# Loading queries, keys and factors with one 128-row transfer per unit in a fused recurrence and Fourier-mixing kernel

## The chip, the cores and the metric

The kernel runs on one core of one Trainium2 chip. The metric is device time in microseconds (us) of one execution, lower is better. The kernel before took 546.61 us (median of 3 runs, 544.95 to 550.81).

## The reference

Two blocks in a row. The first is a gated linear recurrence over 768 tokens for 4 batches, 8 heads and a head width of 48; the second mixes its output with a two-dimensional Fourier transform and a feed-forward layer.

```python
# q, k, v, f_logit: (4, 8, 768, 48)
f = 1 / (1 + exp(-f_logit))
for t in range(S):
    state = f[:, :, t, :, None] * state + einsum('bhd,bhe->bhde', k[:, :, t], v[:, :, t])
    y[:, :, t] = einsum('bhd,bhde->bhe', q[:, :, t], state)

x = y.transpose(0, 2, 1, 3).reshape(4, 768, 384)
mixed = real(fft(fft(x, axis=1), axis=2))
u = x + mixed
un = (u - mean(u)) / sqrt(var(u) + 1e-6)          # over the last axis
out = u + maximum(un @ w_ch1, 0) @ w_ch2          # 384 -> 1536 -> 384
```

## The kernel before, in words

**Units.** Two heads of one batch make a unit, so that there are 16 units, four to a batch. The host hands queries, keys and factor logits over as one array `qkf` with the tokens innermost: for each unit and each of its two heads 48 rows, and in each row 768 tokens of q, then of k, then of f. On the chip a unit's q, k and f are three tiles of 128 rows by 768 tokens: head 0 in rows 0 to 47, head 1 in rows 64 to 111. Rows 48 to 63 are a gap that the matmuls don't read but that the elementwise operations, which run over rows 0 to 111 at once, do.

**Loads** (`load`, line 162). All are issued by SyncE's queue, in the order of the list of steps. A tile of q, k or f comes by two loads of 48 rows each (line 180). The gap of each buffer is filled once, at the start: the factors' four buffers with 30.0 on GpSimd (line 137), the seven buffers of keys and queries on VectorE (`gap`, line 132). There are four buffers for factors (`g_t`), three for keys (`k_t`) and four for queries (`q_t`), used in turn. The values' tile has six chunks of 128 tokens; it comes by three loads, and in its last three chunks the two halves of 64 tokens change places (lines 169 to 171).

**Attention** (`attention`, line 332, and `outputs`). For a unit: exponential and logarithm of the factors on ScalarE (lines 340, 341), a running sum over the tokens on VectorE that starts anew at each chunk (`W`, line 347), the decay over each chunk into `deep` (line 348 for five chunks on VectorE, line 349 for the sixth on GpSimd), two more exponentials (lines 352, 353), the products with queries and keys on VectorE (line 359, and lines 361 and 362 for keys, in two halves because the second one swaps the halves of its chunks), scores on TensorE (line 370), a causal mask (line 374), then products with values (line 528), the rest of the scores (line 545), the chunk states (lines 565, 573, 582), and a turn of the result into token rows `x` (line 602). The keys are turned separately (`keys_turned`, line 507), by a step of their own.

**Token fold** (`fold`, lines 613 to 653). As soon as a unit's part of `x` is there, its token chunks are folded into sums and differences for the Fourier transform. For the last unit of a batch all is on VectorE; for the other three, four of the seven operations (lines 629, 633, 634, 635) are on GpSimd.

**Fourier transform, projections.** When the four units of a batch are folded, `fnet` transforms them (`z`, line 691; `mix`, line 710) and normalizes; `turn` turns the rows for the projections (line 749). `projected` does the two projections for three pairs of token chunks: first 36 matmul calls `up` with the first matrix (line 791), then 42 calls `fx` and `fz` (line 814) with the second, in seven products of blocks. A matmul call in 32-bit floats appears as two instructions in the profile.

**Weights.** The two matrices come as 64-bit floats. Each is loaded in blocks of 384 KB into three `raw` buffers (24 blocks, line 277) and brought to 32 bits by VectorE, ScalarE and GpSimd together (lines 248 to 252). Later they are read a second time into free buffers of keys and factors (`reread`, line 303), for a check of their size.

**The order.** One list of words, `ORDER`, sets the order in which the steps of all this are written, and with it the order on every engine's queue: each engine, SyncE's queue of loads among them, takes its instructions strictly in that order. A number is the next step of that unit, `K` and a number turns that unit's keys, `F`, `H` and `P` with a number are the next step of the transform, the normalization and the projections of that batch, `L` loads (`L12qv`: the queries and values of unit 12), `r` and `R` load blocks of weights, `C` converts one, `V` and `c` read and check them again, `T` loads and `S` sorts the tables of the transform, `D` is eight matmuls without use that keep TensorE's clock up, `I`, `i` and `Z` set constants, `M` is the final judgement of whether a slower, exact path has to follow.

The list was written by a planner outside the kernel. The table loads of `T` (lines 185 to 201) are not touched by the change; one of them, line 199, loads 97 rows of 1,536 bytes.

Of the kernel before, what the change touches and what calls it, by code (L numbers as in the profile page):

```python
# [12 lines left out]
C = 128  # L13
# [6 lines left out]
KEEP = 2.0 ** 20  # L20
# [8 lines left out]
    "I D Gq0 D L0f Gk2 D L1f Gk1 D i D 0 Gk0 D D L0v L0q Gq2 D 1 Gq3 0 D 0 Gq1 D L0k 1 D L1q L2f Z D 1 0 "  # L29
    "D 0 2 K0 L1k D 0 0 2 L2q r L2k 1 D 0 0 L3fk 1 2 L1v D 3 0 K1 1 1 L3q 2 L4fk 0 3 1 L2v 2 C 1 4 r r 1 "  # L30
    "K2 2 2 1 0 4 3 C 2 L5fk 3 L3v D D r 5 2 D 3 2 K3 3 1 3 L4qv 5 4 2 L5qv C 3 4 C 4 R 4 3 D T 5 3 5 K4 "
    "2 L6fk C 5 C S 3 2 3 4 K5 r 3 5 4 D C F0 F0 6 F0 4 6 F0 L6qv C 4 6 F0 r 5 4 r H0 H0 L7fk C r 5 H0 6 "
    "7 5 F0 r P0 6 C C 7 L7qv 5 r K6 P0 P0 7 P0 6 C 7 6 C L8fk r r 5 F0 P0 6 r 6 C 8 C P0 L9fk C r P0 7 6 "
    "P0 9 H0 P0 r H0 7 8 7 C r K7 L9qv P0 r 7 9 C 7 9 6 P0 r L8qv 9 P0 C 9 7 9 C K9 C r P0 P0 8 H0 r 8 P0 "
    "r C L10fk 7 9 8 L11qv C L10qv 9 C 9 10 P0 P0 9 H0 P0 P0 5 W P0 6 L11fk P0 P0 P0 8 7 P0 6 P0 P0 P0 4 "
    "10 8 K8 P0 P0 P0 8 11 7 H0 P0 8 P0 P0 P0 P0 10 P0 P0 P0 P0 10 P0 F1 P0 P0 P0 P0 P0 P0 11 11 F1 L12fk "
    "8 10 K10 P0 P0 12 P0 11 10 F1 P0 F1 P0 L12qv L13fk F1 P0 10 11 H1 10 H1 H1 10 F1 P0 12 13 12 P0 P0 "
    "11 P0 P0 P0 P0 P0 P1 F1 8 P1 H1 L13qv K11 10 9 P1 8 P1 12 P1 P1 P1 H1 11 12 11 H1 P1 12 P1 11 9 P1 "
    "13 K12 P1 P1 P1 13 13 P1 10 P1 11 K13 L14fk P1 V L15fk P1 10 11 P1 P1 12 P1 10 13 15 12 H1 P1 P1 P1 "
    "P1 12 P1 12 L14qv H1 P1 11 P1 11 F2 F2 P1 14 14 P1 F2 13 P1 F2 P1 13 F2 P1 13 H2 V P1 P1 P1 15 14 P1 "  # L40
    "P1 P1 P1 P1 P1 c P1 P1 13 P1 14 14 13 K14 P1 V P1 P1 14 P1 F2 P1 14 P1 P1 H2 c P1 c F2 L15qv P1 P1 "
    "P1 P1 P1 P1 15 V P1 H2 V V H2 14 P1 H2 P2 P2 c P2 P2 P2 c P2 15 14 c 12 P2 V V c c P2 P2 P2 14 15 V "
    "V 13 P2 15 V 15 K15 P2 15 H2 P2 P2 P2 V 15 P2 P2 P2 c P2 13 P2 P2 P2 c P2 14 P2 15 H2 14 P2 P2 P2 V "
    "P2 P2 H2 15 P2 P2 P2 P2 P2 P2 P2 P2 14 c V P2 P2 P2 P2 15 12 c P2 c P2 P2 P2 P2 15 P2 V F3 P2 F3 F3 "
    "c P2 V F3 c c P2 F3 P2 P2 F3 P2 F3 P2 H3 P2 P2 P2 P2 P2 H3 P2 H3 H3 H3 P3 P3 P3 P3 P3 P3 P3 P3 P3 P3 "
    "P3 V P3 P3 P3 P3 H3 P3 P3 V P3 P3 c c P3 P3 P3 V V V c P3 P3 P3 P3 P3 P3 P3 P3 c H3 c H3 P3 P3 V P3 "
    "P3 P3 V P3 P3 P3 P3 P3 P3 P3 c c P3 P3 P3 P3 V P3 P3 P3 P3 P3 P3 P3 P3 c P3 P3 P3 P3 P3 P3 M"
# [7 lines left out]
def kernel(  # L55
# [48 lines left out]
    g_t = [fixed([128, S], f"g{i}") for i in range(4)]  # L104
# [25 lines left out]
    def gap(*tiles, value=0.0):  # L130
        for t in tiles:
            nc.vector.memset(t[32:64], value)

    def start():

        for t in g_t:
            nc.gpsimd.memset(t[32:64], 30.0)
        nc.gpsimd.memset(bound, HIGH)
        nc.gpsimd.memset(bound.rearrange("p (c t) -> p c t", t=C)[:, :, 0:1], LOW)
        nc.gpsimd.memset(low, LOW)  # L140
        nc.gpsimd.memset(eps, 1e-6)
        nc.gpsimd.memset(two, 2.0)
        for t in te_t:
            nc.gpsimd.memset(t, 0.0)
        nc.gpsimd.memset(causal, 1.0)
        for s in range(2):
            half = causal[64 * s:64 * s + 64, :64]
            nc.gpsimd.affine_select(out=half, in_=half, pattern=[[1, 64]], compare_op=ALU.is_ge, fill=0.0,
                                    base=0, channel_multiplier=-1)
# [12 lines left out]
    def load(u, *names):  # L162
        if u >= B * HP:
            return
        b, hp = divmod(u, HP)
        for name in names:
            if name == "v":
                v_of[u] = p3.tile([128, NCH, 2 * D], F32, tag="v", name=f"v{u}")
                nc.sync.dma_start(out=v_of[u][:, :3], in_=v[b, hp, :, :3])
                for s in range(2):  # L170
                    nc.sync.dma_start(out=v_of[u][64 * s:64 * s + 64, 3:],
                                      in_=v[b, hp, 64 - 64 * s:128 - 64 * s, 3:])
                continue
            if name == "V":
                v_of[u] = p3.tile([128, NCH, 2 * D], F32, tag="v", name=f"v{u}")
                nc.sync.dma_start(out=v_of[u], in_=v[b, hp])
                continue
            t, i = {"f": (g_t[u % 4], 2), "k": (k_t[u % 3], 1), "q": (q_t[u % 4], 0)}[name]
            for r in (1, 0):
                nc.sync.dma_start(out=t[ROWS[r]], in_=qkf[b, hp, r, :, i])  # L180
# [117 lines left out]
    def reread():  # L298
        i = len(second)
        t = (k_t[1], g_t[1], k_t[2], g_t[2])[i % 4].bitcast(U32)  # L300
        _, src, cols = blocks_of[i]
        if wide:
            nc.sync.dma_start(out=t, in_=src.bitcast(U32)[:, 2 * cols.start:2 * cols.stop])
        second.append(t.rearrange("p (n w) -> p n w", w=2))
# [27 lines left out]
    def attention(u, x_all):  # L332
# [4 lines left out]
        Q, K, g = q_t[u % 4][:R], k_t[u % 3][:R], g_t[u % 4][:R]  # L337
        AT, AO = at_t[u % 2], ao_t[u % 2]
        at = lambda a, i, c: a.rearrange("p (c t) -> p c t", t=C)[:, c, i]
# [5 lines left out]
        T, ends = deep[:R, u], slice(0, NCH - 1)  # L345
        W = p2.tile([128, S], F32, tag="W", name=f"W{u}")[:R]
        nc.vector.tensor_tensor_scan(W, g, bound[:R], 0.0, ALU.add, ALU.min)  # L347
        nc.vector.tensor_tensor(T[:, ends], at(g, 0, slice(1, NCH)), at(W, C - 1, ends), ALU.add)
        nc.gpsimd.tensor_copy(T[:, NCH - 1:], W[:, S - 1:S])  # L349
# [4 lines left out]
        te = te_t[u % 2][:R]  # L354
        nc.scalar.activation(te[:, :, ends], T[:, ends].unsqueeze(1).to_broadcast([R, D, NCH - 1]),
# [4 lines left out]
        swap = lambda a: a[:, 3 * C:].rearrange("p (c s t) -> p c s t", c=3, s=2)  # L360
        nc.vector.tensor_tensor(g[:, :3 * C], W[:, :3 * C], K[:, :3 * C], ALU.mult)
        nc.vector.tensor_tensor(swap(g)[:, :, ::-1], swap(W), swap(K), ALU.mult)
# [3 lines left out]
        for c in range(NCH):  # L366
            for s in range(2):
                o, k = c * C + 64 * s, c * C + (64 * s if c < 3 else 64 - 64 * s)
                for r in range(2):
                    nc.tensor.matmul(own[64 * s:64 * s + 64, r, c * 64:c * 64 + 64], lhsT=g[ROWS[r], o:o + 64],  # L370
                                     rhs=Q[ROWS[r], k:k + 64], start=True, stop=True)
# [8 lines left out]
    def attention_by_blocks(u, x_all):  # L380
# [5 lines left out]
        Q, K, g = q_t[u % 4][:R], k_t[u % 3][:R], g_t[u % 4][:R]  # L386
# [124 lines left out]
    def outputs(u, x_all, AT, Q, K, te, T=None):  # L511
# [6 lines left out]
        vt = v_of.pop(u)  # L518
        y, vf = y_out, vt.rearrange("p c e -> p (c e)")
# [4 lines left out]
        def values(c, r, rows, t, weights):  # L524
            g, o = into(c, r), c * 2 * D + r * D
# [3 lines left out]
                             lhsT=vf[rows, o:o + (64 if g == 0 else D)], rhs=weights,  # L529
                             start=new, stop=True, skip_group_check=True)  # L530

        def halves(first, second, t, weights):
            for i in range(NCH // 2):
                for p, c in ((first, i), (second, i + 3)):
                    for r in range(2):
                        values(c, r, p, t, weights(p, r, c))

        if te is not None:
            own, far = AT
            halves(hi, lo, hi, lambda p, r, c: own[p, r, c])  # L540
            ps = ps_a.tile([128, 2, 512], F32, tag="sc", name=f"sc{u}_1")
            for i in range(NCH // 2):
                for p, c in ((0, i), (64, i + 3)):
                    for r in range(2):
                        nc.tensor.matmul(ps[p:p + 64, r, i * 64:i * 64 + 64],
                                         lhsT=K[ROWS[r], c * C + p:c * C + p + 64],
# [9 lines left out]
        else:  # L556
            halves(lo, hi, hi, lambda p, r, c: far[p, r, c % 3])
            halves(lo, hi, lo, lambda p, r, c: own[p, r, c])
# [37 lines left out]
        if te is None:  # L596
            load(u + 4, "q", "V")
# [15 lines left out]
    def fold(u, x):  # L613
# [14 lines left out]
        other = nc.vector if last else nc.gpsimd  # L628
        other.tensor_tensor(f[:, 6:3:-1], x[:, 0:3, ch], x[:, 3:6, ch], ALU.subtract)
        nc.vector.tensor_tensor(f[:, 1:4], x[:, 0:3, ch], x[:, 3:6, ch], ALU.add)  # L630
        nc.vector.tensor_tensor(f[:, 0:8:7], f[:, 1:7:5], f[:, 2:6:3], ALU.add)
        nc.vector.tensor_tensor(f[:, 2:6:3], f[:, 1:7:5], f[:, 2:6:3], ALU.subtract)
        other.tensor_copy(f[:, 1:7:5], f[:, 0:8:7])
        other.tensor_copy(f[0:1, 0], f[0:1, 2])
        other.tensor_tensor(f[0:1, 2:7:4], x[0:1, 0:2, ch], x[0:1, 3:5, ch], ALU.subtract)
# [240 lines left out]
    tile_of = {"k": k_t, "q": q_t}  # L876
    with tc.manual_schedule():
        for word in ORDER.split():
# [5 lines left out]
            elif kind == "K":  # L884
                keys_turned(n, g_t[n % 4][:R])
# [24 lines left out]
            elif kind == "G":  # L910
                gap(tile_of[word[1]][n], value=0.0 if word[1] == "q" else KEEP)
# [14 lines left out]
    with tc.If(again > 0):  # L926
# [7 lines left out]
        gap(*k_t)  # L934
        for t in g_t:
            nc.gpsimd.memset(t[32:64], 30.0)
        nc.sync.dma_start(out=causal.rearrange("p (i n) -> p i n", n=32), in_=sel)
        for u in range(4):
            load(u, *("fkqV" if u < 3 else "qV"))
# [78 lines left out]
```

## Time and profile before

| | |
|---|---|
| runs | 544.95, 546.61, 550.81 us; median 546.61 |
| profiled execution | 549.43 us, of which the span from the first to the last instruction is 547.7 us |
| mean granted TensorE clock | 0.969 of full speed |
| TensorE matmuls | 516.5 us busy, 94% of the span, 5,422 instructions |
| TensorE weight loads | 456.8 us, 83% |
| VectorE | 292.4 us, 53%, 534 instructions |
| ScalarE | 200.3 us, 37%, 529 instructions |
| GpSimd | 99.2 us, 18%, 149 instructions |
| transfers | 44.54 MB; 38.90 MB read from memory, 4.72 MB written |
| loads of `qkf` | 96 of 144 KB each; median 4.0 us (factors), 5.2 (queries), 4.8 (keys) from issue to landing |

How to read it. The shares are means over the whole span, and the stages differ: over the first 150 us TensorE waits now and then and VectorE is the busiest of the others; from then on TensorE is busy without a break. A busy time of TensorE is not time at its peak, since matmuls overlap in the pipeline; where the time of a piece of work matters, the start-to-start times of the chain of work that ended last are better. The DMA share is the mean over the sixteen DMA engines of the core, so that one engine that is always busy counts 0.06.

### The profile page before, as it was taken

What the parts mean: (1) busy time and instruction counts of PE and PEld (TensorE: products, weight loads), DVE (VectorE), ACT (ScalarE), POOL (GpSimd) and SP (SyncE); (2) the same over time, 40 slices, a digit from 0 to 9 for tenths busy, and PEclk for the clock granted to TensorE, in tenths of its full rate; (3) what the DMA queues carried; (4) which work ended last, traced back from release to release, by engine and by line L of the source; (5) the groups of instructions that cost most, each with busy time, mean ns of one, the idle gap of its engine ahead of it and who ended that gap; (6) DMA issues with size and microseconds to landing.
All of it is one profiled execution on the core that took longest, in us unless ns stands there. A gap on an engine that the chain in (4) does not pass through costs nothing.

```text
span 547.7 us, 12758 instructions
## 1 busy us (share of the span) xinstructions
PE 516.5 (94%) x5422; PEld 456.8 (83%) x5422; DVE 292.4 (53%) x534; ACT 200.3 (37%) x529; POOL 99.2 (18%) x149
## 2 busy tenths in 40 slices
PE   6887998999999999999999999999999999999992
PEld 6675777866889899899889899898997888989892
DVE  7859889996754265564354356143264730514141
ACT  6676386873331632443440331413213122030200
POOL 5146634433501000321000000003020000000000
PEclk9888599999999999999999999999999999999997
DMA  7994657776100301213010323202010021120101
GB/s 182 206 240 116 184 137 200 205 216 161 56 4 29 87 4 49 70 42 104 1 30 16 89 87 106 97 1 88 1 57 30 0 82 65 28 89 0 59 0 36
DMA packets 20968, 44.54 MB, mean 81 GB/s; under 512 B 3621, under 2 KB 9318, under 8 KB 20902
## 3 DMA queue, kind: packets, MB, share of 16 engines
q1 hardware_dynamic: 19654, 39.90, 27.2%
q0 software_dynamic: 1104, 3.54, 1.7%
q8 instruction: 44, 0.72, 0.6%
q14 instruction: 22, 0.18, 0.1%
q10 hardware_dynamic: 144, 0.20, 0.1%
HBM read 38.90 MB, written 4.72 MB: 80 GB/s over the span
## 4 chain that ended last, share of the span: by engine, by line
PE 70%; DVE 5%; POOL 1%; DMA 1%; issue 1%; ACT 0%; DVEq 0%; POOLq 0%
PE up L791 29%; PE fx L814 16%; PE fz L814 12%; PE z L691 3%; PE mix L710 2%; PE y L528 2%; PE pt L749 1%; PE y L582 1%; DMA raw<-in_w_ch_dram 1%; PE yt L602 1%; PE po L800 1%; PE ds L565 1%; PE sc L370 1%; PE st L507 1%; DVE w L251 1%
## 5 line engine op out<-in xcount | busy, mean ns | idle before, releaser
L791 PE MATMUL up<-unT,w 128*128 128x256 f32 x864 | 195.6, 381 | 1.4 <-DVE x L769 1.1
L791 PEld LDWEIGHTS up<-unT,w 128*128 128x128 f32 x864 | 161.4, 190 | 23.0 <-PE up L791 1.1
L793 ACT ACTIVATE h<-up 128x256 f32<-128x256 f32 x144 | 54.9, 383 | 177.1 <-PE up L791 162.4
L658 POOL DMA_INDIRECT out_dram<-x,place x16 | 16.6, 1038 | 219.7 <-DVE x L844 166.3
L821 DVE TENSOR_TENSOR s<-h,h 128x768 f32<-128x768 f32 x11 | 10.5, 955 | 67.6 <-ACT h L793 67.6
L814 PE MATMUL fx<-block,h 128*128 128x192 f32 x264 | 46.5, 326 | 0.0
L814 PE MATMUL fx<-w,h 128*128 128x192 f32 x264 | 44.9, 326 | 0.0
L814 PEld LDWEIGHTS fx<-w,h 128*128 128x128 f32 x264 | 43.3, 190 | 0.3
L814 PEld LDWEIGHTS fx<-block,h 128*128 128x128 f32 x264 | 43.5, 190 | 0.0
L252 POOL TENSOR_TENSOR w<-w,raw 128x384 uint32<-128x384 uint32 x24 | 28.4, 1183 | 36.3 <-ACT raw L248 16.9
L347 DVE TENSOR_TENSOR_SCAN W<-g,bound 112x768 f32<-112x768 f32 x16 | 28.0, 1753 | 12.9 <-ACT g L341 12.4
L374 DVE COPY_PREDICATED at<-causal,sc 128x768 f32<-128x768 uint32 x16 | 16.6, 1040 | 18.8 <-PE sc L370 18.6
L814 PE MATMUL fz<-block,h 128*128 128x192 f32 x132 | 23.3, 327 | 0.1
L814 PE MATMUL fz<-w,s 128*128 128x192 f32 x132 | 23.3, 327 | 0.0
L814 PE MATMUL fz<-w,h 128*128 128x192 f32 x132 | 23.3, 327 | 0.0
L750 ACT COPY unT<-pt 128x384 f32<-128x384 f32 x24 | 11.5, 483 | 30.3 <-PE pt L749 30.3
L528 PE MATMUL y<-at,v 64*48 64x64 f32 (+1 forms) x768 | 19.6, 235 | 2.5 <-DVE at L374 1.5
L359 DVE TENSOR_TENSOR q<-q,g 112x768 f32<-112x768 f32 x16 | 16.9, 1054 | 9.5 <-ACT g L352 9.5
L814 PEld LDWEIGHTS fz<-block,h 128*128 128x128 f32 x132 | 21.7, 190 | 0.3 <-PE fx L814 0.3
L349 POOL COPY deep<-W 112x1 f32<-112x1 f32 x16 | 5.5, 344 | 89.7 <-DVE W L347 89.7
L814 PEld LDWEIGHTS fz<-w,h 128*128 128x128 f32 x132 | 21.7, 190 | 0.0
L814 PEld LDWEIGHTS fz<-w,s 128*128 128x128 f32 x132 | 21.7, 190 | 0.0
(152 smaller groups left out, 785.7 us busy)
## 6 DMA issues: line engine op xcount, KB each, us to landing
raw<-in_w_ch_dram SPq DMA_DIRECT2D x24, 384.0 KB, 4.5
g<-in_qkf_dram SPq DMA_DIRECT2D x32, 144.0 KB, 4.0
q<-in_qkf_dram SPq DMA_DIRECT2D x32, 144.0 KB, 5.2
k<-in_qkf_dram SPq DMA_DIRECT2D x32, 144.0 KB, 4.8
k<-in_w_ch_dram SPq DMA_DIRECT2D x12, 384.0 KB, 4.1
g<-in_w_ch_dram SPq DMA_DIRECT2D x12, 384.0 KB, 3.4
v<-in_v_dram SPq DMA_DIRECT2D x16, 144.0 KB, 3.7
v<-in_v_dram SPq DMA_DIRECT2D x32, 72.0 KB, 3.9
```

What stands on the lines that cost most here:

```text
L252: nc.gpsimd.tensor_tensor(bits, bits, lo, ALU.add)
L347: nc.vector.tensor_tensor_scan(W, g, bound[:R], 0.0, ALU.add, ALU.min)
L359: nc.vector.tensor_tensor(Q, Q, g, ALU.mult)
L374: nc.vector.copy_predicated(AT, causal[:, :64].bitcast(U32).unsqueeze(1).unsqueeze(1).to_broadcast([128, 2, NCH, 64]), own[:, :, :NCH * 64 ...
L528: nc.tensor.matmul(y[FILL[g], c // 3, c % 3 * C + t.start:c % 3 * C + t.stop], lhsT=vf[rows, o:o + (64 if g == 0 else D)], rhs=weights, st ...
L658: nc.gpsimd.indirect_dma_start(out=out.rearrange("b s d -> (b s) d"), out_offset=bass.IndirectOffsetOnAxis(ap=place[:, b, i:i + 1], axis=0 ...
L691: nc.tensor.matmul(z[:, cols], lhsT=src[:, j, lo:hi], rhs=tab[:, t, T % 2, cols], start=(i == 0), stop=(i == len(parts) - 1), skip_group_c ...
L710: nc.tensor.matmul(mix[:, o], lhsT=zz[:rows_of[T], T, PLACES[c]], rhs=cd[:rows_of[T], T, :NQ - odd], start=(i == 0), stop=(i == 1))
L750: nc.scalar.copy(turned[j][:, :, t], pt[:, :DM].rearrange("p (k t) -> p k t", k=3))
L791: nc.tensor.matmul(pp[:, :256], lhsT=w1[:, kt, m * 128:(m + 1) * 128], rhs=unT[:, kt], start=(kt == 0), stop=(kt == 2))
L793: nc.scalar.activation(hs[-1][:, m % H].rearrange("p t n -> p (t n)"), pp[:, :256], AF.Relu)
L814: nc.tensor.matmul(out, lhsT=h[:, m], rhs=blocks[i][:, m], start=(start and m == 0), stop=(m == H - 1), skip_group_check=True)
```

## The change

Queries, keys and factors of a unit come by one load each instead of two. It reads 64 rows for each head, of which the last 16 belong to the next head, so that the gap holds other data of the same kind and need not be filled; these rows are read twice in all. The destination is all 128 rows of the tile. The source is an access pattern written by hand with an outermost step of two (the heads), then 64 rows, then 768 tokens. For the very last unit, where 16 rows more would leave the array, two loads of 64 and 48 rows stay.

The factors' tiles get one more column, of zeros, so that the sixth chunk's decay is formed by the same VectorE operation as the other five. The keys' product is one operation, since the halves of the values' chunks no longer change places; instead the values come whole by one load, and half of their last three chunks is loaded a second time into rows 64 to 127 of an extra tile `vx` with three buffers. The token fold of all units is on VectorE. The list of steps is new. It has the same steps but for the seven `G` words that filled the gaps, with loads and steps in other places; below are its first line, the lines with the loads of units 8 to 14, and its last line.

```diff
-    "I D Gq0 D L0f Gk2 D L1f Gk1 D i D 0 Gk0 D D L0v L0q Gq2 D 1 Gq3 0 D 0 Gq1 D L0k 1 D L1q L2f Z D 1 0 "
+    "L0f Z L1f I 0 D D L0q D 0 i D 1 1 D 0 L2f L0k 0 D D D r L0v D D C L1q D 2 D L2k 0 D L1k D 1 0 2 1 r "
...
+    "5 r 6 P0 P0 5 6 C 6 K6 r C P0 r H0 C 6 r P0 P0 P0 7 r C P0 6 r H0 C r P0 6 C 7 H0 r P0 C r 7 6 C r C "
+    "P0 7 6 7 K7 r P0 L9fk L8qv C L9qv 7 C 6 L8fk C 7 5 P0 9 4 5 9 P0 P0 7 8 P0 P0 9 P0 P0 8 8 L10fk P0 9 "
+    "7 9 L10qv K9 H0 P0 P0 8 P0 9 P0 P0 P0 9 8 9 H0 9 L11fk P0 W P0 9 K8 8 10 P0 11 10 P0 11 8 7 P0 8 6 "
+    "11 P0 P0 P0 6 L11qv P0 11 P0 P0 8 10 P0 P0 7 P0 P0 P0 7 F1 F1 L13qv P0 F1 10 L13fk K10 F1 P0 10 10 8 "
+    "L12fk F1 P0 10 11 L14fk H1 H1 P0 P0 12 F1 P0 10 H1 P0 P0 14 P0 P0 L12qv 10 12 P0 P0 12 P0 P0 P0 P1 "
...
-    "P3 P3 V P3 P3 P3 P3 P3 P3 P3 c c P3 P3 P3 P3 V P3 P3 P3 P3 P3 P3 P3 P3 c P3 P3 P3 P3 P3 P3 M"
+    "P3 P3 P3 c P3 P3 P3 c M P3 P3 P3 P3 P3 P3 P3 P3 P3 P3 P3 P3 P3"
...
-    g_t = [fixed([128, S], f"g{i}") for i in range(4)]
+    g_t = [fixed([128, S + 1], f"g{i}") for i in range(4)]
...
-            nc.gpsimd.memset(t[32:64], 30.0)
+            nc.gpsimd.memset(t[:, S:], 0.0)
...
-                v_of[u] = p3.tile([128, NCH, 2 * D], F32, tag="v", name=f"v{u}")
-                nc.sync.dma_start(out=v_of[u][:, :3], in_=v[b, hp, :, :3])
-                for s in range(2):
-                    nc.sync.dma_start(out=v_of[u][64 * s:64 * s + 64, 3:],
-                                      in_=v[b, hp, 64 - 64 * s:128 - 64 * s, 3:])
+                v_of[u] = (p3.tile([128, NCH, 2 * D], F32, tag="v", name=f"v{u}"),
+                           pr.tile([128, NCH // 2, 2 * D], F32, tag="vx", name=f"vx{u}"))
+                nc.sync.dma_start(out=v_of[u][0], in_=v[b, hp])
+                nc.sync.dma_start(out=v_of[u][1][64:], in_=v[b, hp, :64, 3:])
...
-            for r in (1, 0):
-                nc.sync.dma_start(out=t[ROWS[r]], in_=qkf[b, hp, r, :, i])
+            rows = qkf.rearrange("b h r d i s -> (b h r d) i s")
+            first = 2 * D * u
+            if u < B * HP - 1:
+                both = bass.AP(tensor=rows.tensor, offset=rows[first:, i].offset,
+                               ap=[[D * 3 * S, 2], [3 * S, 64], [1, S]])
+                nc.sync.dma_start(out=t[:, :S], in_=both)
+            else:
+                nc.sync.dma_start(out=t[:64, :S], in_=rows[first:first + 64, i])
+                nc.sync.dma_start(out=t[64:R, :S], in_=rows[first + D:first + 2 * D, i])
...
-        nc.vector.tensor_tensor(T[:, ends], at(g, 0, slice(1, NCH)), at(W, C - 1, ends), ALU.add)
-        nc.gpsimd.tensor_copy(T[:, NCH - 1:], W[:, S - 1:S])
+        nc.vector.tensor_tensor(T, g_t[u % 4][:R, C::C], W[:, C - 1::C], ALU.add)
...
-        nc.vector.tensor_tensor(g[:, :3 * C], W[:, :3 * C], K[:, :3 * C], ALU.mult)
-        nc.vector.tensor_tensor(swap(g)[:, :, ::-1], swap(W), swap(K), ALU.mult)
+        nc.vector.tensor_tensor(g, W, K, ALU.mult)
...
-        other = nc.vector if last else nc.gpsimd
-        other.tensor_tensor(f[:, 6:3:-1], x[:, 0:3, ch], x[:, 3:6, ch], ALU.subtract)
-        nc.vector.tensor_tensor(f[:, 1:4], x[:, 0:3, ch], x[:, 3:6, ch], ALU.add)
+        tt = nc.vector.tensor_tensor
+        tt(f[:, 6:3:-1], x[:, 0:3, ch], x[:, 3:6, ch], ALU.subtract)
+        tt(f[:, 1:4], x[:, 0:3, ch], x[:, 3:6, ch], ALU.add)
...
-        other.tensor_copy(f[:, 1:7:5], f[:, 0:8:7])
-        other.tensor_copy(f[0:1, 0], f[0:1, 2])
-        other.tensor_tensor(f[0:1, 2:7:4], x[0:1, 0:2, ch], x[0:1, 3:5, ch], ALU.subtract)
+        nc.vector.tensor_copy(f[:, 1:7:5], f[:, 0:8:7])
+        nc.vector.tensor_copy(f[0:1, 0], f[0:1, 2])
+        tt(f[0:1, 2:7:4], x[0:1, 0:2, ch], x[0:1, 3:5, ch], ALU.subtract)
```

## The prediction

> **What bounds the kernel now.** First the busy time by stretches (its columns: stretch; length, then busy us and instructions of TensorE's matmuls, its weight loads, VectorE, ScalarE, GpSimd; TensorE's granted clock; share of the sixteen DMA engines; GB/s).
>
> ```profile
> 0.00:50.00 50.00, 38.08 (x938) 33.11 (x942) 38.20 (x55) 34.71 (x69) 20.78 (x46) 0.89 0.84 185
> 50.00:100.00 50.00, 45.38 (x741) 36.86 (x741) 45.57 (x82) 30.70 (x86) 24.67 (x34) 0.84 0.66 180
> 100.00:150.00 50.00, 48.59 (x603) 36.96 (x596) 41.98 (x67) 26.30 (x66) 22.00 (x26) 1.00 0.55 153
> 200.00:537.00 337.00, 334.62 (x2626) 306.40 (x2624) 143.32 (x283) 89.04 (x255) 29.10 (x41) 1.00 0.16 48
> ```
>
> From 200 us TensorE is full (334.62 of 337) and nothing else matters; the first 150 us are a start-up in which VectorE (up to 45.57 of 50) and the transfers (0.84) are dense. So the time is the moment from which TensorE never waits again, plus the work it then has left, plus the tail. That work is read in the chain of waits (start, length, piece):
>
> ```profile
> 508.13 15.54 PE up L791 x72
> 523.67 3.90 PE fx L814 x24
> 527.57 3.90 PE fz L814 x24
> 531.47 1.95 PE fx L814 x12
> 533.42 1.95 PE fz L814 x12
> 535.37 1.96 PE fx L814 x12
> ```
>
> One pair of chunks costs 15.54 + 13.66 = 29.2 us. In the same chain a unit's attention sums to 5.2 us, a batch's transform to 9.6, a turn to 0.45: 485 us in all, of 547.7.
>
> Third, the transfers, because the change makes them new. One load of before has a row count (97) that shares no divisor with 16: `wave`, line 199. First SyncE's timeline, GpSimd's and two narrow stretches, then the landing times (count, KB, us) of the factors' loads that SyncE issued just behind it and of all factors' loads.
>
> ```profile
> 54.11 0.25 SPq L199 DMA_DIRECT2D wave<-in_dim_tab_dram  x1
> ...
> 64.86 0.46 POOL L211 COPY cd<-wave 97x192 f32<-97x192 f32 x1 [3.60 <-DMA wave<-in_dim_tab_dram]
> ...
> 63.00:64.00 1.00, 1.00 (x20) 0.97 (x19) 0.90 (x4) 0.00 (x0) 0.00 (x0) 0.50 0.06 23
> 64.00:65.00 1.00, 1.00 (x11) 0.81 (x9) 0.93 (x3) 0.00 (x0) 0.14 (x1) 0.50 0.07 26
> ```
> ```profile
> g<-in_qkf_dram SPq DMA_DIRECT2D x2, 144.0 KB, 8.6
> g<-in_qkf_dram SPq DMA_DIRECT2D x32, 144.0 KB, 4.0
> ```
>
> At 63 to 65 us only `wave` moves: share 0.06 to 0.07 is one engine of sixteen, 23 to 26 GB/s. Its 149 KB took until 64.86, 10.7 us after issue. And what was queued behind it landed in 8.6 us instead of 4.0: a load is ready when its slowest engine is, and every load's share waits in that engine's queue. The page adds how many engines each load used:
>
> ```profile
> DMA packets 20968, 44.54 MB, mean 81 GB/s; under 512 B 3621, under 2 KB 9318, under 8 KB 20902
> ```
>
> The 3,621 smallest packets are the completion marks, one per load and engine. Let each load use the largest number up to 16 that divides its outermost count: of SyncE's 215, five have one row (5), five 15 rows (75), one each 97 (1), 63 (9) and 33 rows (11), and 202 use 16 (3,232); GpSimd's 17 make 272, ScalarE's one 16. The sum is 3,621 exactly.
>
> **The change, part by part.**
>
> *Loads.* 47 loads of 393,216 bytes. The destination's outermost count is 128, the source's is 2 (heads, then 64 rows). No load of before differs on its two sides, so the trace leaves two ends: sixteen engines, 393,216 / 16 / 25 GB/s = 0.98 us of each engine, or two engines, 7.86 us of those two. I take two: in the 97-, 63- and 33-row rows every engine took an equal number of outermost rows, and two can't be shared by more than two. Which two is open too; I take always the same, as the loads behind `wave` met on its one engine.
>
> The Trainium skill ("DMA: Bandwidth & Descriptors", section "Why a DMA increments its semaphore by 16 and not by 1") says that the engine count must divide the slowest dimension of both sides, and that SyncE's loads take the lowest-numbered engines. Its section "Rules for kernel authors" speaks for the change instead: two transfers to disjoint partition halves should be one of 128 partitions. The count above agrees with the first; by the second alone the sum would be the second rival's below.
>
> So these two engines become a queue that every load passes, in SyncE's order. In the new list the critical load is unit 12's queries: it stands behind 44 of the 47, after the keys of unit 14. The queue up to it:
> - 44 x 7.86 = 346 us
> - 24 blocks of weights, 393,216 / 16 / 25 = 0.98 each: 23.6
> - values of 13 units, 369 KB each with the second copy, 0.92: 12
> - tables, mostly `wave` at 6: 7.6; start until the first bytes: 2.3
> - a hole: eleven blocks of weights stand before unit 9's factors, and each needs a `raw` buffer back. Before, 14 were issued from 74.88 to 119.10, 3.2 us apiece; landing (3.0 at best), VectorE (0.40 + 0.71) and GpSimd (1.18) over three buffers give 1.8. At 2.5, eleven take 27.5, 10.8 of it counted: 17 more. Bounds 0 and 24.
>
> Sum 408.5. About 2 us more to land and two products (line 359, 1.05, and the keys', the same size) give 412.5 for unit 12's first scores. Buffers don't delay it: unit 14's keys need unit 11's buffer, whose last scores come 38.7 us of TensorE work after its first (landed about 340), at 383, before the queue gets there (388).
>
> What TensorE has left behind these scores, counted in the new list: 297 of 432 `up` calls, 8.25 pairs x 15.54 = 128.3; 378 product calls, 9 pairs x 13.66 = 122.9; attention 25.2 (units 12 to 15 and the end of 10 and 11); two transforms 19.2; 16 turns 7.2. Sum 303. In 153.8 to 537.4 us of before TensorE was busy 381.1 of 383.6, so 305. Before, unit 12's first scores stood at 228.6 us in the chain. Little can fill the wait, since every engine takes its list in order: ScalarE, waiting for unit 7's factors, holds the copies of batch 0's transform listed behind them, and TensorE, waiting for a unit's scores, holds the projections.
>
> *Clock.* The granted clock was 0.50 from 50 to 66 us, amid waits, and 1.00 after 68. One long wait at 384 to 412 costs some 2 us of it.
>
> *Tail.* The judgement (`M`) moves ahead of the last nine `P` steps. Its chain ran from 537.83 to 539.74 with all engines waiting for it: -1.9 from a tail of 10.3.
>
> *VectorE and GpSimd.* The folds of 12 units move 0.45 + 0.26 + 0.20 + 0.35 = 1.26 us each to VectorE (its own rows for lines 629, 633 to 635), 15 us; the keys' product saves 0.60 + 0.66 - 1.05 = 0.2 x 16; seven memsets of 0.70 go. GpSimd loses 34 us of folds and 5.5 of copies. All of it lies under the wait for loads; without that cover, some five folds before 150 us cost up to 6 us there, less the 3.9 us that VectorE waited for GpSimd's part. The sixth column costs VectorE nothing visible (five columns: 0.25 us). The gap's memsets delayed the first loads by at most 2 us, gone now.
>
> **Sum.** 412.5 + 305 + 2 + 8.4 = 728 us of span; the profiled execution is 1.7 longer than its span and the median of the runs 2.8 below it, so 727, said as **727 us**.
>
> Ends: at 26 GB/s the 44 loads cost 13 less, without the hole 17 less; then unit 8's loads decide (about 275, with 387 us of work behind) at some 680. Lower by 20 for work that TensorE finds early: 660. At 23 GB/s 30 more, the hole 7 more, a second late unit some 30: 795.
>
> **Rivals.**
> *Sixteen engines, all hidden (not slower).* The split follows the 128 destination rows. A load then lands like a block of weights (384 KB, 4.5 us). The place is the first 50 us: 2 us of memsets and 1.9 of tail are gained, 547.7 - 3.9 = 543.8 of span, 543 in the runs' terms; with the 3 us of products 540. For it: engines waited for factors only 3.9 us in all. Against: the equal shares above. It decides if the new loads land within about 5 us.
> *Sixteen engines, not hidden.* The doubled rows add 98 KB per load, 2.0 MB for the 20 tiles loaded in the first 60 us: at 185 GB/s up to 10.6 us, take 8, and 3 for the folds: 552.
> *Two engines, but other ones each time.* Loads take 10 us but overlap; units start some 5 us later each until TensorE's backlog covers it: 575.
>
> **Chances.** Forecast 0.85; hidden 0.06 (half of it over 1% faster); not hidden 0.06 (half of it within 1%); other pairs 0.03. A change under 1% can't be told from none here. The range 660 to 795 holds the forecast's bounds, nearly all of its 0.85. Slower 0.91, same 0.06, faster 0.03.
>
> **What would show it.** Landing times of the new loads of 10 us and, queued, several times that; a DMA share near 0.13 at 50 GB/s over long stretches up to 400 us; waits of ScalarE for factors and of TensorE behind them summing to over 150 us; the last long wait of TensorE at unit 12's scores near 410. Landings near 5 us would make the forecast wrong at its first step; 10 us without queueing, at its second; a last wait elsewhere, in the order of the queue.

## The result, and the profile after

The changed kernel takes 741.8 us (median of 4 runs, 740.23 to 742.13) against 545.8 us (544.6 to 550.81): a ratio of 1.356, 95% interval 1.347 to 1.365. Its profiled execution took 742.13 us with a span of 740.4. The forecast was 727 us, so the kind of loss was right and its size 15 us short.

First the page of the kernel after: the engines' busy time and the transfers.

```profile
PE 540.1 (73%) x5422; PEld 474.7 (64%) x5422; DVE 293.3 (40%) x559; ACT 201.2 (27%) x529; POOL 53.5 (7%) x85
...
DMA packets 19825, 50.27 MB, mean 68 GB/s; under 512 B 2015, under 2 KB 4640, under 8 KB 19760
```

TensorE has the same 5,422 matmuls. It is idle for 740.4 - 540.1 = 200.3 us where it was idle for 547.7 - 516.5 = 31.2, and is 23.6 us longer at its work, because the granted clock is lower amid the waits (0.85 in the mean, 0.969 before). These 169.1 and 23.6 us are the whole difference of the spans. And although 5.7 MB more are moved, the smallest packets, the completion marks, fell from 3,621 to 2,015: fewer engines take part in each load.

Now the busy time by stretches, with the columns of the table shown of before: the length, then TensorE's matmuls and weight loads, VectorE, ScalarE, GpSimd, TensorE's granted clock, the transfers' share of sixteen engines, GB/s.

```profile
24.00:31.00 7.00, 0.00 (x0) 0.00 (x0) 0.96 (x1) 0.00 (x0) 0.00 (x0) 0.50 0.14 54
88.00:94.00 6.00, 0.00 (x0) 0.00 (x0) 0.32 (x1) 0.00 (x0) 0.00 (x0) 0.50 0.13 52
0.00:50.00 50.00, 14.34 (x277) 13.52 (x278) 9.48 (x11) 12.18 (x19) 5.81 (x30) 0.69 0.18 63
50.00:100.00 50.00, 7.65 (x150) 6.19 (x145) 9.20 (x11) 5.83 (x13) 1.02 (x1) 0.54 0.21 72
100.00:150.00 50.00, 25.63 (x544) 22.08 (x544) 15.98 (x32) 15.34 (x36) 4.32 (x6) 0.60 0.36 110
250.00:300.00 50.00, 19.22 (x127) 13.21 (x128) 15.48 (x28) 10.45 (x22) 1.72 (x2) 0.69 0.20 72
410.00:731.00 321.00, 318.49 (x2499) 289.00 (x2500) 137.38 (x292) 82.69 (x243) 11.21 (x11) 0.99 0.15 47
```

In the first two rows nearly everything stands still and the transfers run at 0.13 to 0.14: two engines of sixteen (0.125 of them), where the one-engine load of before showed 0.06 to 0.07. TensorE, busy for 38 of the first 50 us before, is busy for 14, then for 8 of the next 50. Only from 410 us is it full, where before it was full from 200.

SyncE's timeline shows the queue itself (start, length of the issue, line, tile).

```profile
57.74 7.37 SPq L174 DMA_DIRECT2D g<-in_qkf_dram  x1
65.24 7.30 SPq L174 DMA_DIRECT2D k<-in_qkf_dram  x1
72.63 7.32 SPq L174 DMA_DIRECT2D g<-in_qkf_dram  x1
80.06 7.46 SPq L174 DMA_DIRECT2D k<-in_qkf_dram  x1
...
212.97 31.06 SPq L274 DMA_DIRECT2D raw<-in_w_ch_dram  x11
```

An issue that takes some 0.5 us where nothing is queued (0.56 at 109.17) now takes 7.3 to 7.5: SyncE gets rid of a load only as fast as the loads pass, some 7.35 us each by the length of the issues (7.46 from start to start), or 393,216 / 2 / 7.35 us = 26.7 GB/s per engine. Who pays is in the list of waits (waiter, tile and line; what it waited for; us in total, times, longest).

```profile
ACT g L336 <- DMA g<-in_qkf_dram: 117.5, 11, 30.6
PE sc L364 <- DVE g L356: 67.3, 5, 31.1
DVE q L355 <- DMA q<-in_qkf_dram: 56.2, 8, 19.5
```

### The profile page after: what moved, and what is told of

Read it like the earlier page. It is cut to its first block, busy times and chain, and to the rows that moved or that the text cites. A ratio compares the mean times of both kernels' runs of the same rounds, so it can differ in the third digit from the quotient of the medians.

```text
span 740.4 us, 12591 instructions
## 1 busy us (share of the span) xinstructions
PE 540.1 (73%) x5422; PEld 474.7 (64%) x5422; DVE 293.3 (40%) x559; ACT 201.2 (27%) x529; POOL 53.5 (7%) x85
## 2 busy tenths in 40 slices
DMA packets 19825, 50.27 MB, mean 68 GB/s; under 512 B 2015, under 2 KB 4640, under 8 KB 19760
## 4 chain that ended last, share of the span: by engine, by line
PE 45%; DMA 5%; ACT 1%; DVE 0%; issue 0%; SPq 0%; ACTq 0%
PE up L788 19%; PE fx L811 10%; PE fz L811 8%; DMA g<-in_qkf_dram 3%; PE z L688 1%; PE mix L707 1%; DMA out_dram<-x 1%; PE y L522 1%; PE pt L746 1%; DMA out_dram<-x,place 1%; PE y L579 1%; PE yt L599 1%; PE ds L562 1%; PE st L501 0%; PE sc L364 0%; ACT h L790 0%
## 5 line engine op out<-in xcount | busy, mean ns | idle before, releaser
L788 PE MATMUL up<-unT,w 128*128 128x256 f32 x864 | 200.6, 388 | 36.3 <-ACT h L790 33.6
L364 PE MATMUL sc<-q,g 48*64 48x64 f32 x768 | 19.3, 257 | 67.4 <-DVE g L356 67.3
L364 PEld LDWEIGHTS sc<-q,g 48*64 48x64 f32 x768 | 16.9, 167 | 69.7 <-DVE g L356 36.6
L336 ACT ACTIVATE g<-g 112x768 f32<-112x768 f32 x16 | 13.5, 843 | 117.5 <-DMA g<-in_qkf_dram 117.5
L522 PEld LDWEIGHTS y<-at,v 64*48 64x48 f32 (+1 forms) x768 | 17.2, 150 | 32.5 <-issue 30.7
L249 POOL TENSOR_TENSOR w<-w,raw 128x384 uint32<-128x384 uint32 x24 | 26.5, 1107 | 158.4 <-DVE w L248 101.6
L245 ACT ACTIVATE raw<-raw,two 128x384 f32<-128x384 uint32 x24 | 15.5, 655 | 51.9 <-DMA raw<-in_w_ch_dram 51.9
L707 PE MATMUL mix<-cd,zz 96*128 96x192 f32 (+2 forms) x96 | 21.9, 383 | 10.0 <-ACT h L790 9.9
L356 DVE TENSOR_TENSOR g<-W,k 112x768 f32<-112x768 f32 x16 | 16.1, 1007 | 31.5 <-DMA k<-in_qkf_dram 29.6
L570 DVE TENSOR_TENSOR_SCAN stt<-ds,te 112x288 f32<-112x288 f32 x16 | 12.0, 751 | 41.5 <-PE ds L562 41.5
L818 DVE TENSOR_TENSOR s<-h,h 128x768 f32<-128x768 f32 x11 | 10.5, 952 | 40.4 <-ACT h L790 40.4
L707 PEld LDWEIGHTS mix<-cd,zz 96*128 96x128 f32 (+2 forms) x96 | 19.1, 226 | 11.4 <-ACT h L790 10.6
```

Of the source, the lines that this page charges most:

```text
L245: nc.scalar.activation(lo.bitcast(F32), lo, AF.Identity, scale=2.0 ** -51, bias=two)
L249: nc.gpsimd.tensor_tensor(bits, bits, lo, ALU.add)
L356: nc.vector.tensor_tensor(g, W, K, ALU.mult)
L522: nc.tensor.matmul(y[FILL[g], c // 3, c % 3 * C + t.start:c % 3 * C + t.stop], lhsT=vals[rows, o:o + (64 if g == 0 else D)], rhs=weights, ...
L707: nc.tensor.matmul(mix[:, o], lhsT=zz[:rows_of[T], T, PLACES[c]], rhs=cd[:rows_of[T], T, :NQ - odd], start=(i == 0), stop=(i == 1))
L788: nc.tensor.matmul(pp[:, :256], lhsT=w1[:, kt, m * 128:(m + 1) * 128], rhs=unT[:, kt], start=(kt == 0), stop=(kt == 2))
```

## The experiments

**1. Two loads of 64 rows: only the form of the loads undone.**

```diff
-                nc.sync.dma_start(out=t[:, :S], in_=both)
+                for r in range(2):
+                    nc.sync.dma_start(out=t[64 * r:64 * r + 64, :S], in_=rows[first + r * D:first + r * D + 64, i])
```

> The kernel after, with each of the 47 loads written as two loads of 64 rows, one per head. The bytes (rows read twice), the new list, the folds and the values' second copy stay; only the source's outermost count changes, from 2 to 64. Theory (a load uses as many engines as divide both outermost counts, so the 128-row load has two): the queue goes, and the time falls to what the other parts make, 540 to 556 us; 142 more completion marks at least, landings near 5 us. Rival (the doubled bytes, the new list or the moved folds lose the time): above 700 us. A time of 560 to 600 would split the loss between the two.

(The trace has 45 such loads, 15 each of queries, keys and factors; "47", here and in the prediction, was a miscount. Unit 12's queries are the 44th, as counted.)

Measured: 547.19 us (12 runs), 0.9996 of before, interval 0.996 to 1.003. From its page, and its transfers (count, KB each, us from issue to landing):

```profile
DMA packets 21176, 50.29 MB, mean 92 GB/s; under 512 B 3365, under 2 KB 5990, under 8 KB 21110
```
```profile
g<-in_qkf_dram SPq DMA_DIRECT2D x31, 192.0 KB, 6.6
q<-in_qkf_dram SPq DMA_DIRECT2D x31, 192.0 KB, 5.8
k<-in_qkf_dram SPq DMA_DIRECT2D x31, 192.0 KB, 4.8
```

The completion marks rise by 3,365 - 2,015 = 1,350 = 45 x (2 x 16 - 2): sixteen marks for each of two loads in place of two for one. All of the loss goes with the form of the load; the doubled rows, the folds on VectorE, the values' second copy and the new list are worth nothing that can be measured, taken together.

**2. One load of 128 rows that follow each other.** One size changed: the source's outermost count, from 2 to 128.

```diff
-                nc.sync.dma_start(out=t[:, :S], in_=both)
+                nc.sync.dma_start(out=t[:, :S], in_=rows[first:first + 128, i])
```

> The kernel after, with each load still one DMA of 393,216 bytes to 128 partitions, but from 128 rows that follow each other, so that the source too has 128 as its outermost count. It computes on other data: the second head's partitions hold rows that lie 16 further on; every instruction and size is the same. Theory (two engines because the source's outermost count is 2): as with two loads of 64, 540 to 556 us. Rival (one large load to 128 partitions is slow in itself, by its size or by being one DMA): near 740 us.

Measured: 540.17 us, 0.985 of before, interval 0.980 to 0.990. From its page:

```profile
DMA packets 20455, 50.27 MB, mean 92 GB/s; under 512 B 2645, under 2 KB 5270, under 8 KB 20390
```

2,645 - 2,015 = 630 = 45 x 14 more marks. Neither the size of the load nor its being one is slow. This version is even a little faster than anything else here; but it computes on other data, and the versions below that put sixteen engines on the right data don't repeat the gain.

**3. The form of the load alone, in the kernel before.** The same access pattern in before's `load`, with before's list, folds and values.

> The kernel before, with its own list, folds and values, and only the loads of queries, keys and factors of 15 units in the 128-row form. Theory: the two engines pass the loads at 7.35 us each, as the issues of the kernel after show. Unit 12's queries are the 39th of them in this list (44th in the new one): 39 x 7.35 = 287 us, some 35 for weights, values and tables, and a hole of up to 24; then 309 us of TensorE work and the tail: 650 to 730 us, likeliest 690. Rival (the loss needs the new list or the folds): near 546 us.

Measured: 730.52 us, 1.334 of before, interval 1.326 to 1.341. The loss needs nothing else of the change; it came half a microsecond above the upper end of what was expected. The critical item was not unit 12's queries: TensorE's last wait over 3 us ended at 321.0, 407 us before the end. Its timelines of GpSimd, VectorE and TensorE show a chain:

```profile
317.33 1.05 POOL L665 DMA_INDIRECT out_dram<-x,place  x1 [24.68 <-DMA out_dram<-x]
319.25 0.36 DVE L638 TENSOR_TENSOR eo<-eo 128x192 f32<-128x192 f32 x1 [20.92 <-POOL eo L636]
320.98 0.92 PE L535 MATMUL y<-at,v 64*48 64x64 f32 x24 [14.87 <-DVE at L381]
```

A store of batch 0's rows, issued by SyncE at 306.89 behind the loads, landed at 316.5. GpSimd's next store waited for it, a fold on GpSimd stood behind that store, VectorE's part of the fold behind GpSimd's, the mask of scores behind the fold, and TensorE behind the mask.

**4. The form for the factors only.** 15 loads in the 128-row form; keys and queries as in experiment 1.

> The kernel after, with the 128-row form for the factors alone (15 loads); keys and queries by two loads of 64 rows. Theory (a queue on two engines): 15 x 7.35 = 110 us of these two engines, of which some 45 in the first 60 us, where they also carry a share of 0.84 of everything else: 555 to 600 us, likeliest 575. Rival (each such load only lands late, without holding up others): 3 to 5 us above the kernel with all loads of 64 rows.

Measured: 609.28 us, 1.114 of before, interval 1.108 to 1.120. That is 62 us above experiment 1, where loads that are only late, each by itself, were to cost 3 to 5: so it is a queue. (That a third of the loads makes a third of the 195 us is no proof of it, since only what ends in a wait of TensorE counts.) My 575 was too low. The delay builds up ahead of the eleven blocks of weights that SyncE issues in a row with no free buffer for them. They begin at 129.85 us, 44 later than in experiment 1 (86.16), and take as long (25.43 against 25.91). Factors issued behind them at 171.15 reached ScalarE, by its timeline, only here:

```profile
184.54 0.84 ACT L339 ACTIVATE g<-g 112x768 f32<-112x768 f32 x1 [13.42 <-DMA g<-in_qkf_dram]
```

TensorE's last long wait, which this ended, was over at 188.7, 57 us later than the same wait in experiment 1 (131.8); from there it was 415 us to the end, against 413. Which term of my sum was short stays open.

**5. and 6. Four groups of 32 rows, sixteen groups of 8.** The same access pattern by hand, overlapping as in the change, with another outermost count:

```diff
-                               ap=[[D * 3 * S, 2], [3 * S, 64], [1, S]])
+                               ap=[[24 * 3 * S, 4], [3 * S, 32], [1, S]])
```
```diff
-                               ap=[[D * 3 * S, 2], [3 * S, 64], [1, S]])
+                               ap=[[6 * 3 * S, 16], [3 * S, 8], [1, S]])
```

> The kernel after, with the source of each large load written as 4 groups of 32 rows, the groups 24 rows apart, in place of 2 groups of 64 rows 48 apart: still one load of 393,216 bytes with overlapping rows. It computes on other data (rows in another order); every instruction and size is the same. Theory (the source's outermost count is the number of engines): 4 engines, 45 x 2 = 90 more completion marks than the 2,015 of the kernel after, issues in the queue 3.7 us apart, 44 x 3.7 + some 45 us = 208 us for unit 12's queries, when TensorE wants them at about 229: only the start-up suffers, 555 to 600 us, likeliest 570. Rival (overlapping or two-level sources are slow whatever the count): near 740 us.

> As the run with 4 groups, with 16 groups of 8 rows, 6 rows apart; other data again. Theory: 16 engines, 630 more completion marks than the kernel after, as with 128 rows in a row: 538 to 548 us. Rival (overlapping or two-level sources are slow whatever the count): near 740 us.

Measured: with 4 groups 608.55 us (1.112, interval 1.106 to 1.117); with 16 groups 550.65 us (1.0065, interval 1.001 to 1.012). SyncE's timeline with 4 groups:

```profile
28.56 3.61 SPq L174 DMA_DIRECT2D g<-in_qkf_dram  x1
32.29 3.53 SPq L174 DMA_DIRECT2D k<-in_qkf_dram  x1
35.92 3.56 SPq L174 DMA_DIRECT2D g<-in_qkf_dram  x1
```

The load passes in half the time of the change (3.6 us against 7.35), and the page counts 2,105 marks, 90 = 45 x 2 more. With 16 groups it counts 2,645, 630 more. So the outermost count of the source sets the number of engines, at 2, 4 and 16 against a destination of 128, and an overlapping two-level source is not slow in itself: 742, 609 and 551 us for one load of the same bytes. Both times lie above what was expected, by 9 and 3 us; with 4 groups the last long wait is again for factors behind the eleven blocks of weights.

**7. Batch 0's last plain store issued by GpSimd, and 9. by ScalarE.** These two test where the forecast's missing 12 us of span are. In the kernel after, TensorE's last wait over 3 us ends at 410.11, at the transform of batch 1 (`mix`), and not at unit 12's scores. ScalarE's timeline names the cause, a copy into batch 2's `x` tile that has batch 0's buffer and waits for that batch's store; below it VectorE's two products of unit 12 and TensorE from the wait on.

```profile
409.07 0.40 ACT L603 COPY x<-yt 128x288 f32<-128x288 f32 x1 [11.66 <-DMA out_dram<-x]
```
```profile
407.64 0.96 DVE L355 TENSOR_TENSOR q<-q,g 112x768 f32<-112x768 f32 x1 [12.64 <-DMA q<-in_qkf_dram]
408.69 0.96 DVE L356 TENSOR_TENSOR g<-W,k 112x768 f32<-112x768 f32 x1
```
```profile
410.11 2.93 PE L707 MATMUL mix<-cd,zz 97*128 97x193 f32 x8 [9.94 <-ACT h L790]
412.98 1.53 PE L579 MATMUL y<-q,stt 48*48 48x128 f32 x20
414.44 1.19 PE L501 MATMUL st<-ident,g 112*128 112x112 f32 x5
415.43 8.67 PE L788 MATMUL up<-unT,w 128*128 128x256 f32 x30
...
424.75 0.90 PE L364 MATMUL sc<-q,g 48*64 48x64 f32 x48
```

SyncE issued that store at 398.88, behind unit 12's loads. Unit 12's scores had their data at 409.65; they stood 14.6 us of work behind `mix` in TensorE's list.

```diff
-            queue = nc.scalar if (b, c) == (B - 1, 0) else nc.sync
+            queue = nc.scalar if (b, c) == (B - 1, 0) else nc.gpsimd if (b, c) == (0, 4) else nc.sync
```
```diff
-            queue = nc.scalar if (b, c) == (B - 1, 0) else nc.sync
+            queue = nc.scalar if (b, c) in ((B - 1, 0), (0, 4)) else nc.sync
```

> The kernel after, with one change: the plain store of batch 0's last chunk (three pieces) is issued by GpSimd and no longer stands in SyncE's list behind unit 12's loads. Theory (the last long wait of TensorE was ScalarE's copy into batch 2's x, which waited for this store, and 14.8 us of listed TensorE work came between it and unit 12's scores): the wait ends some 9 us earlier, at about 401, and the time falls to 730 to 735 us. Rival (unit 12's queries, landed at 407.6, set the end): the wait goes to unit 12's scores, and the time stays at 740 to 743 us.

> The kernel after, with the plain store of batch 0's last chunk issued by ScalarE. From GpSimd it stood behind an indirect store that had to land first, and left only at 401.8 us. On ScalarE it stands behind neither SyncE's loads nor that store. Theory (TensorE's last long wait is for this store, and 14.8 us of listed TensorE work then comes before unit 12's scores): the wait ends by about 401, unit 12's scores come at 415 to 417, and the time falls to 731 to 736 us. Rival (unit 12's queries set the end, whatever the store does): 740 to 743 us.

Measured from GpSimd: 742.3 us, no change, and no test: the store waited there for an indirect store to land, left at 401.79, and the copy still waited for it until 408.12. Measured from ScalarE: 735.11 us, 1.343 of before, interval 1.337 to 1.349, against 1.356 for the kernel after. TensorE's timeline of that run:

```profile
400.82 2.86 PE L788 MATMUL up<-unT,w 128*128 128x256 f32 x12 [3.22 <-ACT h L790]
406.28 2.93 PE L707 MATMUL mix<-cd,zz 97*128 97x193 f32 x8 [2.60 <-ACT h L790]
...
419.65 0.90 PE L364 MATMUL sc<-q,g 48*64 48x64 f32 x48
```

The store is issued at 399.0, no earlier than by SyncE, since in both kernels it first waits for an indirect store to land. But the copy follows 6.2 us behind it, where it was 10.2 in the kernel after: the store was held on its way behind SyncE's loads, not at its issue. The wait does not end by 401 but in two pieces, the second at 406.28, as ScalarE itself now stands still for 6.4 us before the store; unit 12's scores come at 419.65, 5.1 us earlier, and the span is 5.7 us shorter. From the scores to the end of TensorE's work it is 308.0 us in both kernels, and 307.5 in experiment 7. (There the scores came 1.7 us earlier than in the kernel after, at 423.07, and TensorE ended 2.2 us earlier; the tail then took 10.5 us in place of 7.6, the last store's issue alone 2.73 in place of 0.38, so that nothing was gained.) So the moment of these scores sets the end, and the store behind the loads set that moment.

**8., 10. and 11. One load on sixteen engines, on the right data.** A unit's 96 rows do follow each other in memory; only the tile's gap stands between the heads. With head 0 on partitions 16 to 63 the gap lies ahead of both, and one load of 96 rows fills partitions 16 to 111. The first head's products contract over 64 rows, 16 of them fixed values against zeros of the queries.

```diff
-                nc.sync.dma_start(out=t[:, :S], in_=both)
+            nc.sync.dma_start(out=t[64 - D:R, :S], in_=rows[2 * D * u:2 * D * (u + 1), i])
...
-                    nc.tensor.matmul(own[64 * s:64 * s + 64, r, c * 64:c * 64 + 64], lhsT=g[ROWS[r], o:o + 64],
-                                     rhs=Q[ROWS[r], o:o + 64], start=True, stop=True)
+                    nc.tensor.matmul(own[64 * s:64 * s + 64, r, c * 64:c * 64 + 64], lhsT=g[FILL[r], o:o + 64],
+                                     rhs=Q[FILL[r], o:o + 64], start=True, stop=True)
```

> The kernel after, with head 0 on partitions 16 to 63 in place of 0 to 47, so that a unit's 96 rows, which follow each other in memory, are one load of 96 rows (295 KB, nothing read twice); partitions 0 to 15 hold fixed values, zeros for the queries, and the first head's products contract over 64 rows. Theory (96 is divisible by 16 on both sides, so sixteen engines, and fewer bytes than with 128 rows in a row): 535 to 545 us. Rival (the doubled rows cost nothing, and fewer loads bring nothing that the run with 128 rows in a row did not get from its other data): 545 to 550 us, as with two loads of 64.

> The kernel before, with its own list, folds and values, and only the loads changed: head 0 on partitions 16 to 63, and a unit's 96 rows in one load. Against the same loads with the new list and the folds on VectorE it weighs all the rest of the change. Theory (the rest is worth what lies before 50 us and the tail of 1.9 us, so next to nothing): 540 to 547 us, within 1% of that run's 545. Rival (the new list and the folds gain 1 to 2% that the loads gave back): 550 to 556 us.

> The kernel after with head 0 on partitions 16 to 63, and 112 rows in a row per load (16 of them not used) in place of 96: 7 rows per engine in place of 6. It asks why 128 rows in a row (8 per engine) gave 0.985 of the time before, while 16 groups of 8 and loads of 64 or 96 rows gave 0.997 to 1.007. Theory (the engines move rows faster when a load gives each of them more rows that follow each other): 540 to 544 us, in spite of 17% more bytes. Rival (it was the other data or the chip's state of that run): 545 to 549 us.

Measured against before: 545.17 us, 0.997 (interval 0.992 to 1.001), with the new list and folds; 547.13 us, 0.999 (0.996 to 1.002), in the kernel before; 546.15 us, 0.998 (0.995 to 1.000), with 112 rows. All three are the time before. One load per unit in place of two costs nothing when it has sixteen engines, and gains nothing here either; the new list and the folds are worth 0.2%, inside the intervals. No version was shown to beat the kernel before and compute the reference.

## Why the prediction was right, and where it was short

**Two engines per load: right, and shown.** The trace of before had no load whose two sides differ, so this was the step with the two far ends, 0.98 and 7.86 us. The marks of six kernels (2,015, 2,105, 2,645 twice, 2,915 with the factors alone, 3,365) fit two, four and sixteen engines to the last mark. The Trainium skill ("DMA: Bandwidth & Descriptors", section "Why a DMA increments its semaphore by 16 and not by 1") has the engine count divide the slowest dimension of both sides; the runs with counts of 2, 4, 16 and 128 in the source agree with it. Its advice in "Rules for kernel authors" to use one transfer of 128 partitions in place of two halves cost nothing with 128 rows in a row (0.985, on other data) and cost 1.356 with a source of two groups. The prediction lets that section speak for the change; another of its rows, on using all 16 engines, speaks against it: an outermost dimension of fewer than 16 confines a transfer to at most that many engines.

**Always the same two, hence a queue: right.** SyncE's issues of 7.3 us and more show a queue, and so do unit 12's queries: issued from 381.16, they were used at 407.64, 26.5 us later, where one load passes in 7.35. The share stays at 0.13 to 0.14 while loads wait, so it is always two engines that carry them, and the rival of a new pair for each load (575) falls. The marks don't name the engines. Of the forecast's signs, the landing times can't be read, since the page gives none for these loads, and 0.13 alone held only for stretches of 6 to 7 us; means over 50 us are 0.18 to 0.36, as other loads pass too.

**The queue up to unit 12's queries: 410.5 predicted with the landing, 407.6 measured.** Two sizes were off and nearly cancel. A load took 7.35 us and not 7.86, which over 44 loads is 22 us less. Against that, the eleven blocks of weights took 31.06 us instead of 27.5, and "Buffers don't delay it" was wrong: SyncE issued nothing from 342.4 to 355.1, ahead of unit 13's keys, which by the list get unit 10's buffer. That the terms cancel is luck.

**Unit 12's first scores at 412.5: the step that failed, by 12.3 us.** Their data were ready at 409.65, earlier than predicted; they came at 424.75. The sum took the landing of the load as the moment of the scores. It had seen that engines held at their lists would hold work behind them, but not that SyncE's queue holds stores too: one of them held ScalarE, ScalarE held `mix`, and `mix` and 30 `up` instructions were listed ahead of the scores. Experiment 9 shows it by taking 5.1 of the 12.3 us away; the rest is read from the order of TensorE's timeline and was not taken away by a run. In the sum this one term is the whole miss: the span is 12.4 us longer than the 728 predicted. The median lies 2.4 us further off than that, since I took 2.8 us off the profiled execution for it, and here they agree within 0.4.

**What remains after the scores: right in sum.** 305 + 2 + 8.4 = 315.4 predicted, 315.65 measured: 308.0 of TensorE and a tail of 7.6 from its end at 732.8. The 2 us for the clock were lost, but not here:

```profile
410.00:425.00 15.00, 14.89 (x128) 12.46 (x132) 4.30 (x10) 4.59 (x17) 0.00 (x0) 0.68 0.00 1
425.00:450.00 25.00, 24.67 (x262) 23.05 (x253) 17.16 (x35) 8.56 (x22) 0.19 (x1) 1.00 0.13 37
```

At 0.68 granted from 410 to 425 the 30 `up` instructions took 8.67 us against 30 x 15.54 / 72 = 6.5 at full clock, and they stand ahead of unit 12's scores, so these 2.2 us are part of the 12.3. Behind the scores the clock was 1.00, TensorE's work took 3 us more than 305 and the tail 0.8 less than 8.4. That the sum is met to 0.3 us is luck.

**The rest hidden: right, and more so.** The folds, the doubled rows, the second copy and the memsets were said to lie under the wait for loads; experiment 1 takes this cover away and they still cost nothing (0.9996). The rival "sixteen engines, all hidden" gave 540 to 543 and "not hidden" 552: with two loads it is 547, with one load of 128 rows in a row 540.

## What to carry to other kernels

Ask of every load how many engines it can have, from the outermost counts of both sides, before asking how many bytes it has; the count of completion marks on the page answered it exactly in these kernels, and a DMA share that stays at a small multiple of 1/16 while all engines wait for loads is the sign of too few. Two loads whose counts divide by sixteen are far better than one whose source begins with a two. And when a queue slows down, follow everything that passes it: here the last wait, in two different kernels, was for a store that stood behind loads.

## What was not expected

At a full share of the engines the rate depended on how the source is laid out. The tables of stretches of experiment 1 (64 rows), 2 (128 rows in a row) and 6 (16 groups of 8):

```profile
5.00:10.00 5.00, 5.00 (x50) 5.00 (x49) 3.39 (x3) 4.52 (x8) 0.78 (x4) 1.00 0.96 261
20.00:30.00 10.00, 6.59 (x159) 5.47 (x157) 8.16 (x10) 7.13 (x16) 1.01 (x1) 0.85 1.05 255
```
```profile
5.00:10.00 5.00, 5.00 (x59) 5.00 (x58) 4.05 (x5) 4.53 (x7) 0.78 (x4) 1.00 1.02 374
20.00:30.00 10.00, 4.90 (x147) 3.76 (x148) 8.23 (x10) 7.53 (x17) 1.00 (x1) 0.97 0.96 326
```
```profile
5.00:10.00 5.00, 5.00 (x65) 5.00 (x64) 3.01 (x3) 4.46 (x8) 0.78 (x4) 1.00 1.05 261
20.00:30.00 10.00, 6.43 (x157) 5.58 (x161) 7.81 (x11) 7.29 (x16) 1.02 (x1) 0.76 1.04 271
```

326 to 374 GB/s with 128 rows in a row, 255 to 271 with the others, at shares of 0.96 to 1.05; before, with 48 rows per load, it was 222 from 20 to 30 us at 1.04. Loads of 96 and 112 rows in a row (experiments 8 and 11) lie between, at 299 and 292 from 5 to 10 us with shares of 1.05 and 1.04. This may be why the doubled rows cost so little, as the larger loads move more in the same engine time; no run tests it. Nor is the higher rate shown to be what makes experiment 2 faster: the execution with 374 GB/s took 546.43 us, the longest of its five. Experiment 11 asked whether more rows in a row per engine make the difference (7 in place of 6), and found no gain, so why 128 rows in a row are faster stays open.
